# Gathers issued one by one behind pieces of work, and two gate products moved behind a layer, in a fused attention and mixture-of-experts kernel

## The chip, the cores and the metric

The kernel runs on one core of one Trainium2 chip. The metric is the time of one execution on the device in microseconds (us); of several executions the median is given. PE is the matrix engine, DVE the vector engine, ACT the scalar engine, POOL the engine that here issues the indirect transfers (gathers and scatters), SP the engine that issues the plain transfers.

## The reference, cut to what matters

A banded attention gives 3072 tokens of 512 numbers; each token then goes to one of eight experts, and its result is multiplied by a gate.

```python
x = attention(q, k, v, n_global, n_local)        # (4, 8, 768, 64) -> (3072, 512)
logits = x @ w_gate                              # (3072, 8)
expert_idx = np.argmax(logits, axis=1)
gate_w = softmax(logits)[np.arange(N), expert_idx]
for e in range(E):                               # the tokens of expert e, sorted together
    h = np.maximum(x_sorted[lo:hi] @ w1[e], 0.0) # 512 -> 1024
    y_sorted[lo:hi] = h @ w2[e]                  # 1024 -> 512
return gate_w[:, None] * y                       # y back in the tokens' order
```

Everything is in float32.

## The kernel before

`banded_attention()` computes the attention in 48 units and writes the tokens to `x_tok` in DRAM. While it ends, the tokens are counted and sorted by expert, and expert 0's work begins; then a loop goes over the eight experts (`p` from 0 to 7). The order on each engine is the order in which the code is written, since both parts stand under a manual schedule; engines wait for each other where data need it.

**Tokens of an expert** come by gathers. One gather (`gather_one`, L284) is one POOL instruction that fetches 32 tokens, as 128 rows of 128 numbers, with a list of row numbers (`rows_0`, `rows_s`). DVE then turns them (`turn_x`, L295, one transpose for a gather) into the layout that PE reads (`xe`). Expert 0 has place for 464 tokens. Its first 256 come in two halves `z` of 128 at the end of the attention; the other 208 ("the quarter", 7 gathers into `xq_0`) are worked on by the expert loop as `p = 0`. Expert 1 has place for 416 tokens, 13 gathers into `xq_s`.

**Expert 0's first 256 tokens** are a list `fill` of 16 pieces: eight of the first layer (`early_hidden`, L347, each 16 PE rows in the trace, with a relu on ACT, L349) and then eight of the second layer (`early_result`, L354, each 4 rows). `work(n)` does the next `n` pieces. The tail of `banded_attention` puts them between the steps of the sorting, so that PE has work while DVE sorts: `fetch_0(1)` makes the list of row numbers of the quarter and of expert 1 and issues the quarter's seven gathers, `order()`, `settle()`, `identify()`, `sort_acc()` and `fit()` order the other experts by their number of tokens, and `gates_of()` spreads the gates (`gslot`) to the layout of 32-token pieces (`gpc_s`, `gpc_0`): a multiplication on DVE (L276), a product on PE (L279) and a copy on DVE (L280). After the last piece of each half, `scaled()` (L335) evicts it with its gate into a tile `y`, and the scatter of that tile (L327, on POOL) is held back in the list `later`.

After the attention, `take(1)` issues expert 1's 13 gathers one after the other, and then the scatters in `later` are issued.

**The expert loop.** `ground()` (L1013 to L1019) is a check on DVE. `sort(p, part, parts)` is the transposes of an expert's gathers. `hidden(p)` is the first layer: eight products into `ph` (L1065, each 8 rows in the trace, three PSUM buffers), each with a relu on ACT (L1067). `result(p)` is the second layer; for `p = 0` it is `along_row` (four products, L1102, each evicted into `yT` by DVE, L1104, and later transposed back by PE, L1096, within `hidden(1)`); for the others L1119, with L1128 for a last rest. `fetch(p, 0)` (L256) has SP load the first weights of expert `p` as soon as `hidden(p - 2)` has ended, and `fetch(p, 1)` (L1044) the second weights after `result(p - 2)`.

From expert 2 on the gathers are not issued at once: `plan(p)` puts them in the list `pending`, and `pace(n, after)` issues the next `n` of them so that each waits for the instruction `after`, a relu or an eviction of the expert that is being worked on:

```python
def pace(n, after):
    for _ in range(min(n, len(pending))):
        behind(gather_one(*pending.pop(0)), after, "spreads the gathers over the experts' work")
```

Of the kernel before, what the change touches and what calls it, by code (L numbers as in the profile page):

```python
# [8 lines left out]
F32 = mybir.dt.float32  # L9
# [7 lines left out]
P = 128  # L17
# [6 lines left out]
NQ = 4  # L24
# [5 lines left out]
def kernel(  # L30
# [241 lines left out]

    def gates_of(pool, ps, nm, ns, gs, to):

        mg = pool.tile([P, NS, TB], F32, tag="mw", name="mg" + nm, bufs=1)[:, 0:ns, :]
        nc.vector.tensor_tensor(out=mg, in0=gs.rearrange("p (s o) -> p s o", o=1).to_broadcast([P, ns, TB]),  # L276
                                in1=grp.rearrange("p (o g) -> p o g", o=1).to_broadcast([P, ns, TB]), op=ALU.mult)
        pg = ps.tile([P, NS * TB], F32, tag="m", name="pg" + nm)[:, 0:TB * ns]
        nc.tensor.matmul(pg, lhsT=sel, rhs=mg.rearrange("p s g -> p (s g)"), start=True, stop=True)  # L279
        nc.vector.tensor_copy(out=to, in_=pg)  # L280

# [6 lines left out]
    def gather(xq, cols, n, top=N):  # L288
        for i in range(n):
            gather_one(xq, cols, i, top)  # L290
# [8 lines left out]
    def plan(p):  # L299
        if p < E:  # L300
            r = ORDER[p] - 2
            xqs[p] = xq_s[p % 2]
            cols = rows_0[1][:, 2 * TB:] if p == 1 else rows_s[:, NQ * TB * r:NQ * TB * r + NQ * TB]
            for i in range(pieces_of(CAPS[ORDER[p]])):
                pending.append((xqs[p], cols, i))

# [4 lines left out]
    def pace(n, after):  # L311

        for _ in range(min(n, len(pending))):
            behind(gather_one(*pending.pop(0)), after, "spreads the gathers over the experts' work")

    def take(p):
        plan(p)
        while pending:
            gather_one(*pending.pop(0))

# [21 lines left out]
    def hidden_0(ph, q, f0, nf):  # L342

        for f in range(nf):
            c0 = P * (f0 + f)
            for kc in range(KC):
                nc.tensor.matmul(ph[:, P * f:P * f + P], lhsT=w1_0[:, 0, kc, c0:c0 + P], rhs=xe_0[:, kc, P * q:P * q + P],  # L347
                                 start=(kc == 0), stop=(kc == KC - 1))
        nc.scalar.activation(hT_0[q][:, f0:f0 + nf, :], ph.rearrange("p (f s) -> p f s", f=nf), AF.Relu)  # L349

    def result_0(po, q, f0, nf, later=None):

        for fc in range(f0, f0 + nf):
            nc.tensor.matmul(po, lhsT=hT_0[q][:, fc, :], rhs=w2_0[:, 0, fc, :],  # L354
                             start=(fc == 0), stop=(fc == FC - 1))
        if f0 + nf == FC:
            scaled(f"y_0_{q}", P, po, gslot_0[0][:, q:q + 1], idx_0[0][:, q:q + 1], later)

    def distances(dist, kpos, loc):
# [16 lines left out]
    def banded_attention():  # L376
        with ExitStack() as actx:
# [271 lines left out]
            def fetch_0(i):  # L649

                rows_of(ps_m, f"_0{i}", LOTS[i], st.pop(("w", i)), rows_0[i])
                for h in range(2):
                    n = TB if i == 0 else pieces_of(C0) - TB * h
                    gather(xq_0[h], rows_0[i][:, TB * h:TB * h + TB], min(n, TB), N - S if i == 0 else N)

# [7 lines left out]
            def early_hidden(z, f0):  # L663
                ph = ps_s.tile([P, 2, 512], F32, tag="s", name=f"ph_0_{z}_{f0}")
                hidden_0(ph[:, 0, 0:2 * P], z, f0, 2)

            def early_result(z, f0):
                if f0 == 0:
                    st["po"] = ps_o.tile([P, DM], F32, tag="o", name=f"po_0_{z}")
                result_0(st["po"], z, f0, 2, later)  # L670

# [5 lines left out]
            def work(pieces):  # L677

                for _ in range(pieces):
                    do, z, f0 = fill.pop(0)  # L680
                    do(z, f0)

# [143 lines left out]
            sort_acc(1, gslot_s)  # L826
            work(1)
            gates_of(gp, ps_m, "_s", NR * NQ, gslot_s.rearrange("p r q -> p (r q)"), gpc_s)
            gates_of(gp, ps_m, "_1", LOTS[1], gslot_0[1], gpc_0)
            fit()  # L830
            work(2)
            turn_x(xe_0, xq_0[0], TB)
# [166 lines left out]
    with tc.manual_schedule():  # L999
        banded_attention()  # L1000

        take(1)
        while later:
            later.pop(0)()


        r2 = recips.rearrange("p a b -> p (a b)")
# [15 lines left out]
        with ExitStack() as ectx:  # L1023
# [31 lines left out]
            def hidden(p, between=None):  # L1055
# [6 lines left out]
                for fc in range(FC):  # L1062
# [5 lines left out]
                    if fc < 2 and between:  # L1068
                        between(2 * fc, 2 * fc + 2)
                    pace(1 if fc < FC - 1 else len(pending), done)  # L1070

# [14 lines left out]
            def along_row(p, C, w2t, hT):  # L1086
# [12 lines left out]
                for dc in range(KC):  # L1099
                    po = ps_o.tile([P, DM], F32, tag="po", name=f"po_{p}_{dc}")  # L1100
                    for fc in range(FC):
                        nc.tensor.matmul(po[:, 0:C], lhsT=w2t[:, 0, fc, P * dc:P * dc + P], rhs=hT[:, fc, 0:C],  # L1102
                                         start=(fc == 0), stop=(fc == FC - 1))
                    pace(2 if dc == 0 else 1, nc.vector.tensor_copy(out=yT[:, dc, :], in_=po[:, 0:C]))  # L1104
                return turn

# [25 lines left out]
            ground()  # L1132
            sort(1, 0, 1)
            hidden(0)
            fetch(2, 0)
            plan(2)
# [77 lines left out]
```

## Time and profile before

| what | value |
|---|---|
| median of 16 runs | 531.52 us (529.99 to 534.02) |
| the profiled execution's own time | 530.79 us |
| its span in the profile | 528.8 us |
| PE busy in the span | 503.4 us (95%) |
| DVE busy | 182.0 us (34%) |
| ACT busy | 127.4 us (24%) |
| POOL busy | 139.2 us (26%) |
| mean granted clock of PE | 0.988 of full speed |

The page cuts the span into 40 slices, 13.2 us each, and gives the busy share of each engine in tenths; its row PEclk is the clock granted to PE. Rows of the timeline give the start, the length, the engine, the line, the operation, its tiles and shapes, and in brackets the idle time of the engine before it with what ended it. "Remote" stands there when the profile shows no event to put the end of a wait down to. "Issue" is time in which the engine waited for nothing that the profile shows. The ends of PE's rows are modelled.

### The profile page before, as it was taken

What the parts mean: (1) busy time and instruction counts of PE and PEld (TensorE: products, weight loads), DVE (VectorE), ACT (ScalarE), POOL (GpSimd) and SP (SyncE); (2) the same over time, 40 slices, a digit from 0 to 9 for tenths busy, and PEclk for the clock granted to TensorE, in tenths of its full rate; (3) what the DMA queues carried; (4) which work ended last, traced back from release to release, by engine and by line L of the source; (5) the groups of instructions that cost most, each with busy time, mean ns of one, the idle gap of its engine ahead of it and who ended that gap; (6) DMA issues with size and microseconds to landing.
All of it is one profiled execution on the core that took longest, in us unless ns stands there. A gap on an engine that the chain in (4) does not pass through costs nothing.

```text
span 528.8 us, 7971 instructions
## 1 busy us (share of the span) xinstructions
PE 503.4 (95%) x3108; PEld 346.6 (66%) x3108; DVE 182.0 (34%) x484; ACT 127.4 (24%) x227; POOL 139.2 (26%) x161
## 2 busy tenths in 40 slices
PE   3899999999999978999999999999999999999992
PEld 2899999999988935975455446545545846545540
DVE  4787797896874423210120020030011011020010
ACT  2776656654641100101001101100100201101100
POOL 5000000000033375243344145335124525310010
PEclk9999999999999979999999999999999999999997
DMA  8989998999918911590815445173372585110000
GB/s 140 161 151 174 232 168 159 240 186 166 324 38 226 258 46 50 118 280 26 193 60 190 115 115 209 45 162 111 122 166 73 198 188 197 32 41 17 1 34 29
DMA packets 145184, 71.95 MB, mean 136 GB/s; under 512 B 126672, under 2 KB 126678, under 8 KB 145136
## 3 DMA queue, kind: packets, MB, share of 16 engines
q1 hardware_dynamic: 137344, 58.16, 48.0%
q0 software_dynamic: 5264, 12.59, 7.4%
q10 hardware_dynamic: 2528, 0.59, 0.7%
q8 instruction: 26, 0.43, 0.4%
q14 instruction: 22, 0.18, 0.1%
HBM read 59.00 MB, written 12.75 MB: 136 GB/s over the span
## 4 chain that ended last, share of the span: by engine, by line
PE 87%; another core or an unknown queue 5%; DVE 4%; DMA 1%; issue 1%; ACT 0%; SPq 0%; POOL 0%; POOLq 0%; ACTq 0%; DVEq 0%
PE ph L1065 28%; PE po L1119 26%; PE o L542 13%; PE s L507 8%; PE px L559 3%; PE ph L347 2%; PE po L1102 2%; PE pt L1128 1%; PE pq L573 1%; DMA num_w<-in_n_local_dram 1%; PE pi L632 1%; DMA vt<-in_v_dram 1%; DVE num_f L79 1%; DVE w_second L524 0%
## 5 line engine op out<-in xcount | busy, mean ns | idle before, releaser
L1067 ACT ACTIVATE hT<-ph 128x416 f32<-128x416 f32 (+4 forms) x64 | 29.5, 467 | 286.6 <-PE ph L1065 175.6
L284 POOL DMA_INDIRECT xq_s<-x_tok,rows_s x72 | 72.6, 1008 | 64.7 <-ACT hT L1067 38.3
L335 DVE TENSOR_SCALAR y<-po,gslot_s 128x512 f32<-128x512 f32 (+1 forms) x17 | 12.8, 751 | 201.1 <-PE po L1119 201.1
L1065 PE MATMUL ph<-xe,w_second 128*128 128x416 f32 (+3 forms) x256 | 79.5, 471 | 0.0
L1065 PE MATMUL ph<-xe,w_first 128*128 128x208 f32 (+3 forms) x256 | 76.7, 458 | 1.8 <-issue 1.4
L1119 PE MATMUL po<-w_second,hT 128*128 128x512 f32 (+1 forms) x176 | 76.2, 592 | 0.0
L1065 PEld LDWEIGHTS ph<-xe,w_second 128*128 128x128 f32 x256 | 48.2, 190 | 29.5 <-issue 10.4
L1065 PEld LDWEIGHTS ph<-xe,w_first 128*128 128x128 f32 x256 | 47.5, 190 | 30.1 <-issue 12.8
L1119 PE MATMUL po<-w_first,hT 128*128 128x512 f32 (+1 forms) x144 | 62.3, 592 | 0.0
L1119 PEld LDWEIGHTS po<-w_second,hT 128*128 128x128 f32 (+1 forms) x176 | 33.2, 189 | 41.3 <-issue 40.7
L284 POOL DMA_INDIRECT xq<-x_tok,rows x15 | 16.8, 1119 | 163.2 <-DVE rows L271 159.3
L542 PE MATMUL o<-vt,e 128*128 128x128 f32 x288 | 53.2, 275 | 0.0
L327 POOL DMA_INDIRECT out_dram<-y,idx_s x17 | 17.2, 1010 | 124.6 <-DVE xe L295 71.7
L1119 PEld LDWEIGHTS po<-w_first,hT 128*128 128x128 f32 (+1 forms) x144 | 27.2, 189 | 34.0 <-issue 33.5
L542 PE MATMUL o<-va,e 128*128 128x128 f32 x240 | 46.6, 276 | 0.9 <-DVE recips L546 0.9
L542 PEld LDWEIGHTS o<-vt,e 128*128 128x128 f32 x288 | 42.4, 192 | 0.1
L507 PE MATMUL s<-qT,kT 64*128 64x128 f32 x384 | 38.5, 285 | 2.3 <-ACT qT L444 2.3
L513 ACT ACTIVATE e<-s 128x1024 f32<-128x1024 f32 (+1 forms) x36 | 33.4, 948 | 27.8 <-PE s L507 27.4
L542 PEld LDWEIGHTS o<-va,e 128*128 128x128 f32 x240 | 36.4, 192 | 1.1 <-issue 1.0
L507 PE MATMUL s<-qT,kA 64*128 64x128 f32 x320 | 34.1, 291 | 2.0 <-ACT kA L428 2.0
L507 PEld LDWEIGHTS s<-qT,kT 64*128 64x128 f32 x384 | 30.1, 196 | 3.5 <-ACT qT L444 2.7
L524 DVE TENSOR_TENSOR e<-e,Wb 128x1024 f32<-128x1024 f32 x24 | 28.8, 1212 | 10.3 <-ACT e L513 10.0
(189 smaller groups left out, 507.8 us busy)
## 6 DMA issues: line engine op xcount, KB each, us to landing
w_second<-in_moe_w_dram SPq DMA_DIRECT2D x16, 512.0 KB
w_second<-in_moe_w_dram SPq DMA_DIRECT2D x4, 2048.0 KB
x_tok<-xr SPq DMA_DIRECT2D x24, 256.0 KB
w_first<-in_moe_w_dram SPq DMA_DIRECT2D x12, 512.0 KB
w_first<-in_moe_w_dram SPq DMA_DIRECT2D x3, 2048.0 KB
vt<-in_v_dram SPq DMA_DIRECT2D x31, 192.0 KB
w_second<-in_q_dram SPq DMA_DIRECT2D x60, 96.0 KB
w_second<-in_k_dram SPq DMA_DIRECT2D x60, 96.0 KB
```

Of the source, the lines that this page charges most:

```text
L284: return nc.gpsimd.indirect_dma_start(out=xq[:, i, :], out_offset=None, in_=x_tok[0:NJ * top, :], in_offset=bass.IndirectOffsetOnAxis(ap=c ...
L327: p = nc.gpsimd.indirect_dma_start(out=to[:, :], out_offset=bass.IndirectOffsetOnAxis(ap=where, axis=0), in_=y[0:rows, :], in_offset=None, ...
L335: done = nc.vector.tensor_scalar(out=y[0:rows, :], in0=po[0:rows, :], scalar1=gs[0:rows, :], scalar2=None, op0=ALU.mult)
L347: nc.tensor.matmul(ph[:, P * f:P * f + P], lhsT=w1_0[:, 0, kc, c0:c0 + P], rhs=xe_0[:, kc, P * q:P * q + P], start=(kc == 0), stop=(kc == ...
L507: nc.tensor.matmul(ps[:, h, P * m:P * m + P], lhsT=lhsT, rhs=qT[r, P * i:P * i + P], start=True, stop=True)
L513: nc.scalar.activation(e[:, :, 0:w], ps[:, :, 0:w], AF.Exp, scale=D ** -0.5)
L524: nc.vector.tensor_tensor(out=eh, in0=eh, in1=W[:, 2 * j:2 * j + 2, P:3 * P].rearrange("p h (o c) -> p h o c", o=1).to_broadcast([P, 2, 2, ...
L542: nc.tensor.matmul(po[:, t, h, :], lhsT=pt[:, h, P * m:P * m + P], rhs=(vt if own else va)[:, c0:c0 + P], start=(m == mine[0][0]), stop=(m ...
L559: nc.tensor.transpose(px[:, 2 * i + t, :], xrs[b, c][:, t, P * j:P * j + P], ident)
L1065: nc.tensor.matmul(ph[:, 0:C], lhsT=w1t[:, 0, kc, P * fc:P * fc + P], rhs=xe[:, kc, 0:C], start=(kc == 0), stop=(kc == KC - 1))
L1067: done = nc.scalar.activation(hT[:, fc, 0:C], ph[:, 0:C], AF.Relu)
L1119: nc.tensor.matmul(po[0:rows, :], lhsT=hT[:, fc, P * q:P * q + rows], rhs=w2t[:, 0, fc, :], start=(fc == 0), stop=(fc == FC - 1))
```

## The change

- `gates_of` no longer does everything at once. It multiplies on DVE into a tile of its own and returns `rest`, which does the product and the copy. It is called in the expert loop, after `ground()`; `rest` is called after `hidden(0)`.
- `fetch_0(1)` puts the quarter's seven gathers into `pending`, issues two of them at once, and plans expert 1's 13 behind them. `work()` calls `pace(1, ...)` after each piece, so each piece of PE's work lets one gather go. The rest goes behind the relus of `hidden(0)`, one behind each; the last relu no longer lets all that are pending go when `p` is 0. `take` is gone.
- `work(1)`, the two `gates_of` and `work(2)` in the tail become one `work(3)` after `fit()`.
- Expert 1's transposes, in one go ahead of `hidden(0)` before, go in two parts behind the second and the third eviction of `along_row`. The two scatters held back in `later` follow them there, one each.

```diff
-    def gates_of(pool, ps, nm, ns, gs, to):
-        mg = pool.tile([P, NS, TB], F32, tag="mw", name="mg" + nm, bufs=1)[:, 0:ns, :]
+    def gates_of(pool, nm, ns, gs, to):
+        mg = pool.tile([P, ns, TB], F32, tag="mg" + nm, name="mg" + nm, bufs=1)
         nc.vector.tensor_tensor(out=mg, ..., op=ALU.mult)
-        pg = ps.tile([P, NS * TB], F32, tag="m", name="pg" + nm)[:, 0:TB * ns]
-        nc.tensor.matmul(pg, lhsT=sel, ...)
-        nc.vector.tensor_copy(out=to, in_=pg)
+        def rest(ps):
+            pg = ps.tile([P, DM], F32, tag="pt", name="pg" + nm)[:, 0:TB * ns]
+            nc.tensor.matmul(pg, lhsT=sel, ...)
+            nc.vector.tensor_copy(out=to, in_=pg)
+        return rest
...
             def fetch_0(i):
                 for h in range(2):
                     n = TB if i == 0 else pieces_of(C0) - TB * h
-                    gather(xq_0[h], rows_0[i][:, TB * h:TB * h + TB], min(n, TB), N - S if i == 0 else N)
+                    for k in range(min(n, TB)):
+                        pending.append((xq_0[h], rows_0[i][:, TB * h:TB * h + TB], k, N - S if i == 0 else N))
+                if i == 0:
+                    while pending:
+                        gather_one(*pending.pop(0))
+                else:
+                    for _ in range(2):
+                        gather_one(*pending.pop(0))
+                    plan(1)
...
                 for _ in range(pieces):
                     do, z, f0 = fill.pop(0)
-                    do(z, f0)
+                    pace(1, do(z, f0))
...
             sort_acc(1, gslot_s)
-            work(1)
-            gates_of(gp, ps_m, "_s", NR * NQ, gslot_s.rearrange("p r q -> p (r q)"), gpc_s)
-            gates_of(gp, ps_m, "_1", LOTS[1], gslot_0[1], gpc_0)
             fit()
-            work(2)
+            work(3)
             turn_x(xe_0, xq_0[0], TB)
             turn_x(xe_0[:, :, P:2 * P], xq_0[1], pieces_of(C0) - TB)
             work(4)
...
         banded_attention()
-        take(1)
-        while later:
-            later.pop(0)()
...
-                    pace(1 if fc < FC - 1 else len(pending), done)
+                    pace(1 if fc < FC - 1 or p == 0 else len(pending), done)
...
                     pace(2 if dc == 0 else 1, nc.vector.tensor_copy(out=yT[:, dc, :], in_=po[:, 0:C]))
+                    if 0 < dc < KC - 1:
+                        sort(1, dc - 1, KC - 2)
+                        later.pop(0)()
...
             ground()
-            sort(1, 0, 1)
+            spread_gates = [gates_of(hp, "_s", NR * NQ, ..., gpc_s),
+                            gates_of(hp, "_1", LOTS[1], gslot_0[1], gpc_0)]
             hidden(0)
+            for do in spread_gates:
+                do(ps_t)
             fetch(2, 0)
             plan(2)
             turn = result(0)
```

## The prediction

> **What bounds the kernel now.** I read the page first, for the engine that is busy nearly always and the slices where it is not. Its rows over 40 slices of 13.2 us:
>
> ```profile
> PE   3899999999999978999999999999999999999992
> PEclk9999999999999979999999999999999999999997
> ```
>
> PE is the bound: outside the first slices and the last one it is below 9 only in slices 14 and 15 (185 to 211 us), and its clock dips in slice 14. So I asked for that stretch in steps of 5 us; columns are busy time of PE, PEld, DVE, ACT, POOL with counts, then granted clock, DMA share, GB/s:
>
> ```profile
> 180.00:185.00 5.00, 5.00 (x32) 3.79 (x31) 1.39 (x5) 0.77 (x2) 3.78 (x5) 1.00 0.77 273
> 185.00:190.00 5.00, 1.96 (x7) 0.74 (x5) 2.05 (x9) 0.00 (x0) 3.78 (x5) 0.87 0.11 32
> 190.00:195.00 5.00, 5.00 (x8) 2.36 (x9) 1.03 (x7) 0.00 (x0) 3.78 (x5) 0.50 0.20 52
> 195.00:200.00 5.00, 5.00 (x12) 2.12 (x11) 1.37 (x5) 0.00 (x0) 3.85 (x4) 0.95 0.18 52
> 205.00:210.00 5.00, 3.32 (x16) 2.44 (x15) 0.75 (x2) 0.53 (x3) 1.02 (x1) 1.00 0.19 66
> ```
>
> PE stands in 185:190, runs "busy" at half clock in 190:195 (8 rows in 5 us) and stands again in 205:210, while POOL issues gathers without a break (3.78 of every 5 us). The timeline of PE names the rows (start, length, line, shape, count, idle before):
>
> ```profile
> 184.34 1.91 PE L354 MATMUL po<-w_first,hT 128*128 128x512 f32 x4
> 186.95 0.46 PE L279 MATMUL pg_s<-mg_s,sel 128*128 128x96 f32 x2 [0.71 <-DVE gslot_s L722]
> 189.75 0.62 PE L279 MATMUL pg<-mg,sel 128*128 128x24 f32 x2 [2.33 <-issue]
> 190.20 13.18 PE L354 MATMUL po<-w_first,hT 128*128 128x512 f32 x24
> 203.22 3.86 PE L1065 MATMUL ph<-xe,w_first 128*128 128x208 f32 x21
> 209.86 7.30 PE L1065 MATMUL ph<-xe,w_first 128*128 128x208 f32 x40 [0.25 <-ACT hT L1067]
> ```
>
> A matmul in fp32 shows as two rows. The two gate products (L279) stand between pieces of expert 0's second layer, and PE waits for DVE around them. The timeline of all engines shows why that takes so long, and why PE stands again before 209.86:
>
> ```profile
> 189.35 0.26 DVE L280 COPY gpc_s<-pg_s 128x96 f32<-128x96 f32 x1 [2.45 <-remote]
> 209.25 0.75 DVE L335 TENSOR_SCALAR y<-po,gslot 128x512 f32<-128x512 f32 x1 [8.49 <-remote]
> 209.47 0.81 ACT L1067 ACTIVATE hT<-ph 128x208 f32<-128x208 f32 x3 [26.21 <-remote]
> ...
> 277.14 0.39 SPq L1044 DMA_DIRECT2D w_second<-in_moe_w_dram  x1
> 277.15 0.35 DVE L1083 TENSOR_SCALAR y_p<-pt,gpc 128x128 f32<-128x128 f32 x1 [3.90 <-remote]
> ```
>
> The gate product ends at 187.41 by its rows, but DVE's copy of it starts 1.9 us later. The last product of the second layer ends at 203.4, its eviction starts at 209.25, and the three relus that were ready from 204.8 on start together at 209.47. Two engines go on within 0.22 us, so it was not DVE that was held but word of PE's work that came late. The same at 277: the piece product ended at 274.35, and SP and DVE, which both wait for it, go on at 277.14 and 277.15. In all these places POOL is in a run of gathers or scatters. What holds the word back, no row shows.
>
> **The change, part by part.** All of it lies in one stretch, from the first row of the second layer (182.42) to the start of expert 0's second product, L1102, at 217.16 (the chain of waits). What PE must do there: 32 rows of L354 at 0.429 us (L1119's 48 such rows take 20.60 us in the chain) is 13.73; the row-number product (184.14 to 184.34) 0.20; 64 rows of L1065 at 0.1825 (40 in 7.30) is 11.68; the gates' two products, from the like pairs of L270 (0.20 and 0.14), 0.34. Sum 25.95 us. The stretch takes 34.74, so 8.79 us are lost, in three places. The gates: PE's piece ends at 186.06 and the next begins at 190.20, 4.14 less 0.34 of work, 3.80. The clock: 24 rows from 190.20 to 203.22 take 13.02 for 10.30, 2.72. The late relus: 24 rows from 203.22 to 209.86 take 6.64 for 4.38, 2.26.
>
> *Gates.* They leave the second layer; their DVE multiplications come after `ground()`, their products after the whole first layer of expert 0's quarter, their copies before the first `yT` copy. No PE row waits for DVE inside the layer any more: the 3.80 go, and with them the clock's 2.72, since the clock fell only after that idle time. The 0.34 of products are paid later and are in my sum. Cover: the multiplications are done by about 201 (eviction after 196.4, some 2.3 us of `ground`, 0.4 of their own), 7 us ahead of need; separate buffers let both products go back to back.
>
> The Trainium skill ("TensorE: Matmul & The Clock Gate", Part 1) has the clock halve after about 3.4 us of idle and return after about 3.4 us of work. Halving after this idle time agrees (0.50 from 189 on), but here the half clock lasts to 195.4; by the page's return the clock's term would be an estimated 1.7, and the time 1.0 us longer than I forecast.
>
> *Second half of expert 0's tokens.* Two gathers go at once, five behind pieces of PE work. PE's pieces last 1.72 us, a gather holds POOL for 1.00 plus 0.30 to the next, so POOL keeps up. The seventh goes behind the piece that ends at 187.8 (187.06 before); a gather issued at 163.49 let its transpose start at 166.05, 2.56 later, so this one lands at about 190.4, and the seven transposes (1.46) are done by 192. PE needs them at 182.42 + 13.73 + 0.20 = 196.35. Cover: 4.3 us, and beyond it each us costs one.
>
> *Expert 1's 13 gathers.* Five go behind pieces (to 196.5), eight behind the relus, one each 1.46 us. Since each is issued after a piece or relu is reported done, POOL is idle for 0.4 to 0.7 us between them and the long run is broken. Behind a waiting gather stand on POOL only more gathers and the two scatters. I take the late relus' 2.26 as gone. Bounds: nothing gone, or all; PE has three `ph` buffers, so a relu may be 2.5 us late at no cost; at 277, after a short run, the word was 2.8 late.
>
> *What is late next.* The first layer ends at 208.03, and at about 208.2 SP, whose queue order is unchanged, issues the load of expert 2's first weights (L256), which waits for just that. The thirteenth gather waits for the last relu and goes at about 208.6: 0.4 us behind the load. The trace has one such case: load at 251.90, gather at 252.69. In the DMA queues' view from 252.5 to 262 (packets, MB, share) the software queue, with a gather's 128 packets and a scatter's asked for, moves 31:
>
> ```profile
> q1 hardware_dynamic: 498, 1.85, 94.1%
> q0 software_dynamic: 31, 0.05, 2.9%
> ```
>
> So it lands when the load is through. The first load (issued 217.20) moves 0.30 MB to 220 and 1.77 MB from 220 to 229, so it takes 11.9 us; here it ends at 220.1. Its transpose (0.27) lets expert 1's first layer start at about 220.5, where PE is ready at 208.03 + 0.34 + 11.25 (L1102) + 0.12 = 219.74. I take a wait of 0.8; bounds 0 (it slips in ahead) and 3 (gathers issued at 220 to 223.5, in mid-load, show software packets mostly after 229, 14 us after the load's issue).
>
> The Trainium skill ("DMA: Bandwidth & Descriptors", Queues, rings and completion order) has each DMA engine take turns between queues packet by packet; by that the gather would land in a few us and the wait be 0. The 31 packets speak against it.
>
> *Transposes and evictions.* Expert 1's 13 transposes (2.63 at 211.64, in one go) move between the `yT` copies: 6 after the second (at about 214.2) and 7 after the third (217.1). DVE is otherwise idle there (0.38 of each 2.8 us). Behind a transposition that waits stands the fourth copy, due at 219.8; nobody needs it until PE's transposes after the first `ph`, 2.9 us on. The two scatters held back leave 205 and 210 for 214 to 218: POOL then has five gathers and two scatters, 7 × 1.3 = 9.1 us, in 11.25.
>
> *Sum.* 8.79 - 0.8 = 8.0 us off the profiled execution's own 530.79 (528.8 span and 2.0 around it), so 522.8. The runs' median, 531.52, is 0.73 above it: I predict 523.5. From 228 on PE is full to the end in the windows, so the gain is carried through.
>
> **The rivals.** *Word from PE stays late.* The gathers still run beside PE, and one run of three POOL operations at 273.5 already delays the word by 2.8. If the relus come as late as now, PE stands 2.26 again: 525.8. For: lateness without a long run. Against: it costs PE nothing at 277, with the same three buffers.
>
> *The gather slips in ahead of the load* (its descriptors are written before the load's data flows, about 1.3 us after issue): 522.7. It lies inside my forecast.
>
> *Slower: the thirteenth gather blocks DVE and PE.* Wait W is paid in full, and beyond about 3.7 us (the idle time after which the clock fell) 2.7 more for the clock. The gain is eaten when W + 2.7 = 8.8, W = 6.1: a landing at 225.6, 17 us after issue. The load would have to last 17 us instead of 11.9, and the longest in the trace is some 14. With 19 us: 533.2.
>
> *The change does not remove the idle time*, because expert 0's transposes come later than 196.35: 4.3 us of cover would have to be used up, by five gathers each late by a late word of 1 us or more. With 5 us more than the cover and the clock lost again: 531.
>
> **How the numbers follow.** Forecast with the slip 0.75, late word 0.14, idle time elsewhere 0.05, slower 0.06. The range takes the wait from 0 to 3 (522.7 to 525.7), the late word on the forecast (525.8) and with part of the wait (527), and below, 1 us for the rows' rounding and the median's own spread: 521.7 to 527. About 0.2% (1.06 us) is what a measurement of this kernel can tell from no change; faster by more 0.91, within 0.03, slower 0.06.
>
> **What would show it.** Right: clock 1.00 from 185 to 210, 24 rows of L354 in one run of 10.3 us, the first relu within 1 us of its product, L1102's successor starting near 208.4, and a wait of about 0.8 for DVE before expert 1's first `ph`. Wrong: PE idle before the first layer of the quarter (cover used up), the first relu still us behind its product (late word), or over 3 us before expert 1's `ph` (the load).

## The result, and the profile after

The changed kernel takes 520.97 us, median of 11 runs (518.75 to 522.94), against 531.61 us for the kernel before in the same series: ratio 0.9793, 95% interval 0.9776 to 0.9809. Forecast were 523.5 us, with a range from 521.7; the time lies 0.7 us below its low end. The profiled execution takes 520.62 us (span 518.8), where 522.8 was worked out.

The rows of PE and of its clock over the 40 slices, from the page of the changed kernel:

```profile
PE   3899999999999999999999999999999999999993
PEclk9899999999999999999999999999999999999998
```

Slices 14 and 15 are full, and the clock's dip is gone. The same stretch in steps of 5 us (busy time of PE, PEld, DVE, ACT, POOL with counts, then clock, DMA share, GB/s):

```profile
185.00:190.00 5.00, 5.00 (x13) 2.28 (x12) 2.11 (x11) 0.00 (x0) 2.21 (x3) 1.00 0.11 29
190.00:195.00 5.00, 5.00 (x13) 2.21 (x12) 1.20 (x7) 0.00 (x0) 3.31 (x4) 1.00 0.14 39
205.00:210.00 5.00, 5.00 (x32) 5.00 (x31) 0.35 (x2) 0.69 (x2) 2.98 (x3) 1.00 0.40 118
```

PE does 13 rows from 190 to 195 where it did 8. Its timeline:

```profile
181.78 1.88 PE L354 MATMUL po<-w_first,hT 128*128 128x512 f32 x4
183.69 12.21 PE L354 MATMUL po<-w_first,hT 128*128 128x512 f32 x28
195.74 11.42 PE L1066 MATMUL ph<-xe,w_first 128*128 128x208 f32 x64
207.36 11.50 PE L1103 MATMUL po<-hT,w_first 128*128 128x208 f32 x64
219.73 3.06 PE L1066 MATMUL ph<-xe,w_second 128*128 128x416 f32 x8 [0.76 <-issue]
```

The second layer and the first layer of the quarter are one row each, with no idle time in brackets. From the start of L354 to the start of the quarter's second product it is 25.58 us (181.78 to 207.36). By the same rows of the kernel before it was 34.58 us:

```profile
182.42 1.88 PE L354 MATMUL po<-w_first,hT 128*128 128x512 f32 x4
...
217.00 11.42 PE L1102 MATMUL po<-hT,w_first 128*128 128x208 f32 x64
```

One wait is new, 0.76 us before expert 1's first layer. The timeline of the other engines shows the eviction and the first relu on time, and where the wait comes from:

```profile
195.94 0.75 DVE L334 TENSOR_SCALAR y<-po,gslot 128x512 f32<-128x512 f32 x1 [4.74 <-PE po L354]
197.47 0.34 ACT L1068 ACTIVATE hT<-ph 128x208 f32<-128x208 f32 x1 [14.86 <-issue]
206.83 0.71 ACT L1068 ACTIVATE hT<-ph 128x208 f32<-128x208 f32 x2 [2.11 <-PE ph L1066]
207.19 1.96 SPq L256 DMA_DIRECT2D w_first<-in_moe_w_dram  x4
208.74 1.00 POOL L288 DMA_INDIRECT xq_s<-x_tok,rows  x1 [0.30 <-issue]
219.36 0.31 DVE L299 STREAM_TRANSPOSE xe<-xq_s 128x128 f32<-128x128 f32 x1 [1.73 <-DMA xq_s<-x_tok,rows]
```

The relus keep PE's step up to the seventh, which starts 1.1 us after its product's end and back to back with the eighth (206.83). The last two gathers wait for these two relus, so the thirteenth goes at 208.74, 1.55 us behind the load, and its transpose waits for it until 219.36.

What is left of the 10 us lies outside the stretch. The changed kernel is 0.65 us ahead already at 159 us, in code that is the same; and it ends faster. The last scatter of the kernel before (span 528.8 us), and then of the changed one (span 518.8 us):

```profile
520.56 0.95 POOL L327 DMA_INDIRECT out_dram<-y,idx_s  x1 [5.88 <-DVE y L335]
```
```profile
511.95 0.95 POOL L326 DMA_INDIRECT out_dram<-y,idx_s  x1 [5.89 <-DVE y L334]
```

From this row to the end of the span it is 8.2 us before and 6.9 after. The trace has POOL go from one closing instruction to the next after a gap of 1.3 us before (524.67 to 525.99) and 0.03 after, and the queue that fetches instructions has one packet more before than after:

```profile
q14 instruction: 22, 0.18, 0.1%
```
```profile
q14 instruction: 21, 0.17, 0.1%
```

### The profile page after: what moved, and what is told of

It reads as the page before. It is cut to its first block, busy times and chain, and to the rows that moved or that the text cites. A ratio compares the mean times of both kernels' runs of the same rounds, so it can differ in the third digit from the quotient of the medians.

```text
span 518.8 us, 7988 instructions
## 1 busy us (share of the span) xinstructions
PE 499.4 (96%) x3108; PEld 345.5 (67%) x3108; DVE 182.2 (35%) x484; ACT 127.0 (24%) x227; POOL 138.0 (27%) x161
## 4 chain that ended last, share of the span: by engine, by line
PE 93%; DVE 3%; DMA 2%; issue 1%; ACT 0%; POOL 0%; POOLq 0%; SPq 0%
PE ph L1066 30%; PE po L1123 26%; PE o L543 14%; PE s L508 8%; PE po L354 3%; PE px L560 3%; PE ph L346 2%; PE po L1103 2%; PE pt L1132 1%; PE pq L574 1%; DMA vt<-in_v_dram 1%; DMA num_w<-in_n_local_dram 1%; PE pi L633 1%; DVE num_f L79 1%; DVE w_second L525 0%
## 5 line engine op out<-in xcount | busy, mean ns | idle before, releaser
L1066 PE MATMUL ph<-xe,w_second 128*128 128x416 f32 (+3 forms) x256 | 79.6, 471 | 0.8 <-issue 0.8
L1066 PE MATMUL ph<-xe,w_first 128*128 128x208 f32 (+3 forms) x256 | 75.8, 457 | 0.1
L1066 PEld LDWEIGHTS ph<-xe,w_second 128*128 128x128 f32 x256 | 48.2, 190 | 30.4 <-issue 11.3
L1066 PEld LDWEIGHTS ph<-xe,w_first 128*128 128x128 f32 x256 | 47.5, 190 | 27.6 <-issue 10.7
```

The lines of the kernel that those rows point to most:

```text
L1066: nc.tensor.matmul(ph[:, 0:C], lhsT=w1t[:, 0, kc, P * fc:P * fc + P], rhs=xe[:, kc, 0:C], start=(kc == 0), stop=(kc == KC - 1))
```

## The experiments

Theory A: a run of gathers that follow each other without room on POOL holds PE's word of finished work; all three losses of the stretch (round the gates, the half clock, the late relus) are that, and pacing the gathers removes them. Theory B, the prediction's own sum: the gates' idle time with the half clock, and the late relus, are separate terms.

The runs were made in five further series, each on one chip. In the first two the kernel before takes 531.9 and 532.7 us, as on record; in the last three 521.9, 521.6 and 521.6. That is a finding of its own (below); each ratio is to the kernel before in its own series. A trace can be up to 1.4 us ahead of another or behind it before the stretch begins (L559 at 153.28 in pad8_before, at 154.45 in the kernel before, at 155.84 in changed_third), so the stretch is counted from its own first row where that matters.

| run | kernel before | this | ratio (95%) |
|---|---|---|---|
| gates_only | 531.88 | 534.28 | 1.0049 (1.0032 to 1.0065) |
| gathers_only | 531.88 | 521.35 | 0.9814 (0.9795 to 0.9833) |
| four_ahead | 531.88 | 519.92 | 0.9784 (0.9765 to 0.9803) |
| pad8_before | 531.88 | 529.63 | 0.9964 (0.9949 to 0.9979) |
| spaced | 532.65 | 520.97 | 0.9794 (0.9762 to 0.9826) |
| run_of_8 | 532.65 | 519.87 | 0.9764 (0.9737 to 0.9792) |
| attn_gathers | 532.65 | 540.19 | 1.0151 (1.0118 to 1.0183) |
| attn_memsets | 532.65 | 520.36 | 0.9781 (0.9751 to 0.9811) |
| spaced_gates | 521.85 | 519.78 | 0.9960 (0.9944 to 0.9976) |
| spaced_short | 521.85 | 520.35 | 0.9971 (0.9959 to 0.9983) |
| run_of_8_again | 521.85 | 519.25 | 0.9951 (0.9934 to 0.9967) |
| changed_again | 521.85 | 519.58 | 0.9961 (0.9948 to 0.9973) |
| before_again | 521.59 | 521.77 | one run |
| spaced_short_again | 521.59 | 520.51 | 0.9981 (0.9966 to 0.9996) |
| changed_third | 521.59 | 519.41 | 0.9962 (0.9943 to 0.9980) |
| run_of_8_third | 521.59 | 519.07 | 0.9953 (0.9937 to 0.9970) |
| spaced_short_third | 521.62 | 520.90 | 0.9978 (0.9962 to 0.9994) |
| gates_only_again | 521.62 | 520.67 | 0.9978 (0.9960 to 0.9996) |

### The gates alone, the gathers alone

```diff
# gates_only, against the kernel before; gates_of as in the change
...
-            work(1)
-            gates_of(gp, ps_m, "_s", ...)
-            gates_of(gp, ps_m, "_1", ...)
             fit()
-            work(2)
+            work(3)
...
             ground()
+            spread_gates = [gates_of(hp, "_s", ...), gates_of(hp, "_1", ...)]
             sort(1, 0, 1)
             hidden(0)
+            for do in spread_gates:
+                do(ps_t)
```

> The kernel before with the gates' part of the change alone: their multiplications after ground(), their products and copies after hidden(0), the pieces in one work(3); the 20 gathers stay in one run without a pause, and expert 1's transposes and the two held-back scatters stay where they were. Theory A (word of PE's work comes only when POOL's run of gathers ends, whatever PE does): the second layer's 32 rows run in one piece to about 196.4, PE fills its three ph buffers by about 200.6 and then stands until the relus' word comes at 207 to 209, as before; expert 0's second product still starts at 215 to 217, and the kernel gains 0 to 2 us (529.5 to 531.6), although the gates' idle time and the half clock behind them are gone or have moved. Theory B (the three losses are separate terms, as the prediction's sum has them): 3.80 and 2.72 go, the relus' 2.26 stays: about 525.1, ratio 0.988.

Measured: slower by half a per cent, 534.28 us. The timeline of PE in gates_only, and then that of the other engines:

```profile
184.93 12.21 PE L359 MATMUL po<-w_first,hT 128*128 128x512 f32 x28
196.97 4.38 PE L1067 MATMUL ph<-xe,w_first 128*128 128x208 f32 x24
211.63 9.15 PE L1067 MATMUL ph<-xe,w_first 128*128 128x208 f32 x40 [10.28 <-ACT hT L1069]
```
```profile
205.85 1.02 POOL L332 DMA_INDIRECT out_dram<-y,idx  x1 [0.30 <-issue]
206.79 0.75 DVE L340 TENSOR_SCALAR y<-po,gslot 128x512 f32<-128x512 f32 x1 [12.71 <-remote]
...
207.82 1.16 POOL L332 DMA_INDIRECT out_dram<-y,idx  x1 [0.95 <-DVE y L340]
...
211.24 0.81 ACT L1069 ACTIVATE hT<-ph 128x208 f32<-128x208 f32 x3 [27.46 <-remote]
```

The second layer runs in one piece, as theory B has it, and nothing is won by it. Its last product ends at 197.1, and DVE evicts it only at 206.79, as POOL's run ends (206.87). PE fills its three `ph` buffers and stands 10.28 us; the relus come at 211.24, behind one more scatter. Against before the second product starts 3.98 us later, which is 1.77 (relus at 211.24 instead of 209.47), 1.85 (40 rows in 9.15 instead of 7.30, since after such idle time the clock is 0.50) and 0.36 for the gates' products. Of the 1.77, 0.59 is that the layer itself begins later in this trace (183.01 for 182.42); counted from there the stretch is 3.39 us longer (37.97). The gain of removing the gates' idle time was paid back at the next wait, which lasts to the run's end. The word is not held for the whole run, though: the first half is evicted at 191.95, in its middle. Theory A forecast that the gain would be gone, though not that it would turn into a loss.

Half clock costs 2.1 us on these 40 rows (7.04 at the 0.176 of the row after). By the granted clock in steps of 1 us (0.79 in 215:216, and 0.74 in 195:196 before) it lasted 3.8 us from PE's restart here, and 5.3 us in the kernel before. The Trainium skill ("TensorE: Matmul & The Clock Gate", Part 1) has the clock return after about 3.4 us of sustained work; both are longer here.

gathers_only is the reverse: the changed kernel with the gates back in `work(1)`, gates, `fit()`, `work(2)`.

```diff
# gathers_only, against the changed kernel; gates_of as before, spread_gates gone
...
+            work(1)
+            gates_of(gp, ps_m, "_s", ...)
+            gates_of(gp, ps_m, "_1", ...)
             fit()
-            work(3)
+            work(2)
```

> The changed kernel with the gates' multiplications, products and copies back between the pieces of expert 0's second layer, in work(1), gates, work(2); the gathers one by one behind pieces and relus, transposes and scatters as in the changed kernel. Theory A (the idle time round the gates was mostly late word of PE's work too): the copy of the first gate product starts within 1 us of its end instead of 1.9, PE's idle time between the pieces falls from 3.80 to 2 or less, the clock stays at 1.00, and the relus are on time: 523 to 525. Theory B (the idle time round the gates is the chain over DVE, whatever POOL does): idle 3.8 and half clock 2.7 stay, only the relus' 2.26 goes, less the 0.8 for the thirteenth gather: about 530.

Measured 0.9814, theory A. PE's timeline in gathers_only:

```profile
185.47 0.46 PE L279 MATMUL pg_s<-mg_s,sel 128*128 128x96 f32 x2
186.37 0.40 PE L279 MATMUL pg<-mg,sel 128*128 128x24 f32 x2 [0.44 <-DVE mg L276]
186.61 10.55 PE L350 MATMUL po<-w_first,hT 128*128 128x512 f32 x24
197.00 11.42 PE L1065 MATMUL ph<-xe,w_first 128*128 128x208 f32 x64
208.25 11.42 PE L1102 MATMUL po<-hT,w_first 128*128 128x208 f32 x64
```

The gates stand where they stood, and PE is idle round them for about half a us (0.11 and 0.44) instead of 3.80; no half clock follows. The stretch takes 26.71 us (181.54 to 208.25): 7.87 of the 9.00 us come from the gathers, with the transposes and scatters that move along with them, and 1.13 from the gates.

### Is it the run, and of what?

```diff
# spaced, against the kernel before: the seven gathers of fetch_0(1) likewise
     def take(p):
         plan(p)
         while pending:
             gather_one(*pending.pop(0))
+            nc.gpsimd.memset(pad, 0.0)          # 256 columns
```

> The kernel before with a memset of 256 columns (some 0.3 us) on POOL behind each of the 20 gathers of the quarter and of expert 1; nothing waits for PE. POOL stays busy without a pause, but a gather starts only every 1.6 us instead of 1.3, and the run ends some 6 us later. Theory A (as long as gathers follow each other with no wait for PE in between, PE's word comes only behind the run): the first relu comes 6 us later than before, PE stands longer, and the kernel is 4 to 7 us slower (ratio 1.008 to 1.013). Theory B (gathers that follow each other at POOL's highest rate hold the word; a little room lets it through): relus on time, gain of 2 to 8 us (0.985 to 0.996).

Measured 0.9794: 20 memsets on the busy engine, with nothing else changed, bring what the whole change brings. (In both, about 1.3 us of that are the end of the kernel, below. The stretch takes 26.78 us in spaced, 181.80 to 208.58, as in gathers_only.) The timelines of POOL and ACT in spaced:

```profile
196.55 1.01 POOL L284 DMA_INDIRECT xq_s<-x_tok,rows  x1 [0.17 <-issue]
197.56 0.33 POOL L321 MEMSET pad<- 128x256 f32 x1
198.05 1.00 POOL L284 DMA_INDIRECT xq_s<-x_tok,rows  x1 [0.17 <-issue]
...
199.06 0.34 ACT L1072 ACTIVATE hT<-ph 128x208 f32<-128x208 f32 x1 [16.68 <-PE ph L1070]
200.34 0.34 ACT L1072 ACTIVATE hT<-ph 128x208 f32<-128x208 f32 x1 [0.94 <-PE ph L1070]
```

A gather starts every 1.49 us instead of 1.30, POOL never pauses, nothing waits for PE, and the relus come in PE's step, beside the run. So it is not the wait for PE that helps, nor POOL's leisure. Whether the 0.19 us or the other instruction does it was to be told by a memset of one column, with a gather still every 1.30 us:

> The kernel before with a memset of one column on POOL behind each of the 20 gathers, in place of 256 columns, so that a gather starts about every 1.3 to 1.4 us. Theory A (the word needs room in time between the gathers; 0.19 us more from one to the next was enough in the run spaced): with little room the word is late again, at least in part: 0.985 to 1.003. Theory B (another instruction between two gathers is what lets it through): 0.978 to 0.981.

> The kernel before with a memset of one column on POOL behind each of the 20 gathers; a gather still starts every 1.30 us. Where the kernel before takes about 531.5 us: theory A (the word needs room in time): late as in the kernel before, ratio 0.995 to 1.003; theory B (another instruction between two gathers lets it through): 0.978 to 0.981. Where the kernel before takes about 522 us it tells nothing, ratio 0.997.

> The kernel before with a memset of one column behind each of the 20 gathers, a gather still every 1.30 us. Where the kernel before takes about 531.5 us: theory A (the word needs room in time): 0.995 to 1.003; theory B (another instruction between two gathers lets it through): 0.978 to 0.981. Where it takes about 521.7 us: 0.997 to 0.998 again, nothing told.

All three fell into series in which the word is not late in the kernel before either; they tell nothing, and this stays open. What they gain, 0.7 to 1.5 us, is about the gap at the end, which none of them has.

The same run elsewhere, and its control, both in the changed kernel (20 unused gathers, or 18 memsets, behind an exponential of the attention at about 105 us):

```diff
+                if n0 == 30:
+                    for i in range(20):
+                        one = nc.gpsimd.indirect_dma_start(out=xq_s[i // 13][:, i % 13, :], in_=<128 rows of moe_w2>, ...)
...
+                    for i in range(18):
+                        one = nc.gpsimd.memset(xq_s[i // 9], 0.0)
```

> The changed kernel with 20 gathers added that nobody uses (128 rows of 128 numbers of the second weights, into the tiles that experts 1 and 2 are gathered into later), in one run on POOL from about 105 us, in the attention, where PE, ACT and DVE wait for each other every few us and POOL has nothing to do. Theory A (a run of gathers holds PE's word, wherever it is): PE's word comes late there too, and since a unit of the attention needs it every 3 us, the kernel is 5 to 20 us slower (ratio 0.989 to 1.018). Theory B (the word is held by something of the stretch around 200 us, not by the run): within 1 us of the changed kernel (0.978 to 0.981).

> The control for the gathers in the attention: the changed kernel with 18 memsets of 1.49 us added on POOL at the same place, 27 us in one run without a DMA. Theory A1 (gathers hold PE's word, POOL's work as such does not): within 1 us of the changed kernel (0.978 to 0.981). Theory A2 (any run of POOL's does, or it takes DVE's access to memory): several us slower, as with the gathers.

The changed kernel has 0.9793. With the memsets it is 0.9781, no difference; with the gathers 1.0151, 19.8 us more than with the memsets on the same chip. Windows of attn_gathers, then of attn_memsets:

```profile
115.00:120.00 5.00, 4.18 (x45) 3.47 (x43) 2.74 (x3) 1.14 (x2) 3.78 (x5) 1.00 1.07 203
120.00:125.00 5.00, 3.12 (x11) 2.33 (x12) 0.00 (x0) 0.00 (x0) 3.78 (x5) 0.65 1.30 205
```
```profile
120.00:125.00 5.00, 5.00 (x58) 4.76 (x57) 3.25 (x6) 2.60 (x4) 4.83 (x5) 1.00 1.04 189
```

From 120 to 125 DVE and ACT do nothing at all while POOL gathers, and PE does 11 rows for 58. POOL's memsets, as long and as dense (4.83 of 5 us), disturb nobody. That it is word of PE here too, and not the loads of the attention, shows in ACT's timeline of attn_gathers: the scores that this exponential reads come from PE alone, their last row ended at 116.45, and ACT takes them up 9.6 us later, after standing idle for 7.51.

```profile
126.04 1.02 ACT L516 ACTIVATE w_second<-s 128x1024 f32<-128x1024 f32 x1 [7.51 <-remote]
```

PE itself is held as well: from 119.6 on its rows start singly, some 0.7 us apart (119.60, 120.32, 121.03), with idle time that the profile puts down to issue. In the kernel before three rows of the first layer start like that too (207.77, 208.47, 209.17).

So it is the gathers, not POOL's being busy, and not something of the place around 200 us. Whether it is their issuing on POOL or what they move, these runs do not separate.

### How long a run is harmless, and the thirteenth gather

```diff
# run_of_8, against the changed kernel
-                    pace(1, do(z, f0))
+                    pace(1 if fill else len(pending), do(z, f0))
# four_ahead, against the changed kernel
-                    for _ in range(2):
+                    for _ in range(4):
                         gather_one(*pending.pop(0))
```

> The changed kernel, but the last piece of expert 0's second layer lets all eight remaining gathers go at once, instead of one behind each relu of the first layer. Theory A (the relus were on time after the change only because each gather waits for a relu): the run of eight, from about 196 to 206.6, holds PE's word of the first products; the first relus come at 207 to 209, PE stands from about 200, ratio 0.990 to 0.996. Theory B (it takes the longer run of before, more than ten gathers, to hold the word): relus within 2.5 us of their products, PE does not stand, and since the thirteenth gather is now ahead of the load, 0.978.

> The changed kernel with four instead of two gathers of the quarter issued without a wait, so that expert 1's thirteenth gather goes behind the sixth relu and not behind the last, ahead of the load of expert 2's first weights. Theory A (the 0.76 us that PE stands before expert 1's first layer is this gather queued behind the load): all 20 gathers are issued by about 206, ahead of the load, the wait is gone, ratio 0.978 to the kernel before (520.2) where the changed kernel has 0.9793. Theory B (a gather is late through POOL's run, or the longer run at the start makes word of PE's work late): same time as the changed kernel or up to 1 us longer (0.979 to 0.981).

run_of_8: 0.9764. ACT's timeline:

```profile
200.66 0.34 ACT L1068 ACTIVATE hT<-ph 128x208 f32<-128x208 f32 x1 [1.06 <-issue]
202.38 0.34 ACT L1068 ACTIVATE hT<-ph 128x208 f32<-128x208 f32 x1 [1.37 <-PE ph L1066]
205.21 0.34 ACT L1068 ACTIVATE hT<-ph 128x208 f32<-128x208 f32 x1 [2.49 <-PE ph L1066]
208.08 0.34 ACT L1068 ACTIVATE hT<-ph 128x208 f32<-128x208 f32 x1 [2.52 <-PE pg L281]
```

The relus now come 1.4 us apart and then 2.8, so the run of eight does hold the word in its second half; but PE's 64 rows take 11.42 us without idle time, since three buffers cover it. Theory A was right that the word is held, though not from the first relu on, and wrong on the price, theory B the other way round. The thirteenth gather goes ahead of the load in both kernels (207.11 for 209.64, and 205.91 for 207.52 in four_ahead), and PE's wait before expert 1 is gone in both traces. four_ahead's ratio is 0.0009 below the changed kernel's, half a us, where 0.76 was expected; the intervals do not separate that from zero.

> The same kernel as in the run run_of_8 (0.9764, interval 0.9737 to 0.9792 from four executions), beside the changed kernel on the same chip. Theory A (it is faster than the changed kernel by the 0.76 us that PE stands behind the thirteenth gather, and late word inside three buffers costs nothing): 0.7 to 0.8 us less than the changed kernel, ratio 0.0014 lower. Theory B (chance): same as the changed kernel within 0.3 us.

> The changed kernel with the last eight gathers let go at once by the last piece of the second layer. Where the kernel before takes about 531.5 us: 0.7 to 0.8 us less than the changed kernel, from the wait that goes; where it takes about 522 us: the same within 0.3 us.

Beside the changed kernel, where the word is not late, run_of_8 is 0.33 and 0.34 us faster (519.25 to 519.58, 519.07 to 519.41), each time less than the intervals can tell. With 0.9764 to the 0.9793 on record it has the lowest median wherever it ran, by little and nowhere clear of the noise.

### Where the instructions lie

```diff
# pad8_before, against the kernel before, at the start of the attention
+        for _ in range(8):
+            nc.gpsimd.memset(pad, 0.0)          # one column
```

> The kernel before with eight memsets of one column added on POOL early in the attention, where POOL is idle; nothing else changes. The trace of before shows 1.3 us between the end of POOL's INC_SWDGE_SEM (524.67) and its last long DRAIN (525.99), with one more fetch of instructions (22 against 21) than after the change, where the gap is 0.03. Theory A (the gap is a fetch of POOL's instructions, and where it falls depends on how many instructions lie ahead): the gap goes or moves, and the time falls by 0 to 1.3 us (ratio 0.9975 to 1.000). Theory B (the gap belongs to the end of the kernel before, or is chance): gap and time stay (ratio 1.000), or the gap is there in some executions only. The 0.65 us that the changed kernel is ahead already at 159 us, in code that is the same, is looked at as well: if it is a matter of the run, it comes and goes in the traces of these four kernels.

Measured 0.9964, 2.2 us by the medians. The gap at the end is gone (0.04 us), with 21 packets of instructions for 22. The 22 packets recur in all four traces of the kernel before and of gates_only, with a gap of 1.2 to 1.3 us, and in none of the other 16 traces. So about 1.3 us of the change's gain come from where POOL's instructions lie, and not from what they do. That the gap goes with the packets is shown; that it is the fetch itself is argued from the one packet. PE's timeline of pad8_before also shows the run's end at work again:

```profile
180.16 1.88 PE L354 MATMUL po<-w_first,hT 128*128 128x512 f32 x4
...
185.23 10.55 PE L354 MATMUL po<-w_first,hT 128*128 128x512 f32 x24
...
207.34 9.35 PE L1068 MATMUL ph<-xe,w_first 128*128 128x208 f32 x40 [4.34 <-ACT hT L1070]
```

Here the word of the gates' products happened to come early: the idle time round them is 0.44 us and the clock stays full, and by the start of the next row of L354 PE is 5.0 us ahead of before (185.23 for 190.20). Of these 2.3 were there when the layer began (180.16 for 182.42), and 2.7 are won at the gates. All but 0.5 us is lost again: the second half, whose last row ended at 195.8, is evicted at 206.73, the first relus come at 206.95, 2.9 us after the run's end (204.05; 3.2 us before), and the second product starts at 216.53 (217.00 before). Counted from its first row the stretch is 1.8 us longer than before (36.37).

### Where the word is not late

> The kernel before, unchanged. Theory A (late word of PE's work shows on some chips only): where the runs of before take about 531.5 us, the trace has the idle time at 185 to 190 and 205 to 210, half the clock in between, and the first relus 3 to 6 us behind their products; where they take about 522 us, the same gathers run at the same 1.30 us, and the relus follow their products within 0.1 us. Theory B (the kernel before was faster there for another cause, such as the start, the loads or the end): the lateness is there in either case.

> The changed kernel itself, beside the others on the same chip: 0.979 again. Its trace shows whether the lead of 0.65 us at 159 us, in unchanged code, and the missing gap at the end come again. Theory A (the gap goes with where the instructions lie): no gap in this trace either. Theory B (chance): gap and lead may be there or not.

> The changed kernel, beside the others on the same chip: 0.979 where the kernel before takes about 531.5 us, 0.996 where it takes about 522 us. In the first case PE stands 0.76 us before expert 1's first layer, in the second not, since with timely relus the thirteenth gather goes ahead of the load.

> The gates' part of the change alone, as in the run gates_only, with the memset of 256 columns behind each of the 20 gathers. Theory A (the gates' idle time was late word too, and what is left of it once the gathers are spaced is about 0.6 us): 0.978 to 0.979, half a us less than with spacing alone (0.9794), although the same move made the kernel slower (1.0049) while the gathers ran without room. Theory B (moving the gates costs something by itself, as gates_only showed): 0.981 to 0.985.

> The kernel of the run gates_only again. Where the kernel before takes about 531.5 us: 1.005 again. Where it takes about 521.7 us: PE's idle time round the gates is 0.5 us there (185.30 to 185.41 and 185.87 to 186.31 in the trace of before_again), and that is the gain, 0.9985 to 0.9995, with the gap at the end still there.

The kernel before, unchanged, takes 521.6 to 521.9 us in these series. From its page, then the timeline of POOL and ACT, then that of PE:

```profile
PE   3999999999999999999999999999999999999992
PEclk9999999999999999999999999999999999999997
```
```profile
196.56 1.00 POOL L284 DMA_INDIRECT xq_s<-x_tok,rows  x1 [0.30 <-DMA xq_s<-x_tok,rows]
...
198.67 0.34 ACT L1067 ACTIVATE hT<-ph 128x208 f32<-128x208 f32 x1 [16.61 <-PE ph L1065]
199.95 0.34 ACT L1067 ACTIVATE hT<-ph 128x208 f32<-128x208 f32 x1 [0.94 <-PE ph L1065]
```
```profile
186.31 0.40 PE L279 MATMUL pg<-mg,sel 128*128 128x24 f32 x2 [0.44 <-DVE mg L276]
196.93 11.42 PE L1065 MATMUL ph<-xe,w_first 128*128 128x208 f32 x64
```

The same 20 gathers run at the same 1.30 us, and no relu is late. By the times of PE's semaphore updates in the ten traces of these three series, one word of PE's comes more than 0.3 us after its product (0.9 us, in spaced_short); in the kernel before on record 22 do, in the changed kernel 18. The stretch takes 26.71 us (181.48 to 208.19), to the hundredth what gathers_only reaches where the word is late. So pacing does all that a chip without this lateness would do, and no more.

What is left there is 0.9961 and 0.9962, 2.2 us: 1.13 of the stretch, which is the gates (26.71 to 25.58 in gates_only_again, 0.9978, 0.95 us by the medians, twice what was expected from the idle time alone), and the gap at the end, 1.2 to 1.3. spaced_gates and the changed kernel are equal there (519.78, 519.58); its stretch takes 25.57 us without idle time, but what it gains over a late kernel before, its question, was not to be had. PE's wait before expert 1 is 0.17 us in changed_third and none in changed_again, but not because the thirteenth gather goes ahead of the load, as was expected: it goes 0.62 us behind it in both (208.74 for 208.12, 207.34 for 206.72).

Whether the chip decides, or the time at which it was used, the runs do not tell: each of the five series was on a chip of its own.

## Why the prediction was right and wrong

**The stretch.** Forecast was 8.79 us, measured 9.00; 64 rows of L1066 take 11.25 instead of 11.68, and the two gate products 0.37 instead of 0.34. Clock, one run of rows, first relu 0.3 us behind its product: the signs named came, with the second product starting 1.0 us ahead of the time named (207.36 for 208.4).

**Why it goes.** Here the working was wrong in a way that the sum did not show. "No PE row waits for DVE inside the layer any more: the 3.80 go, and with them the clock's 2.72" put 6.52 us down to moving the gates. Alone that brings a loss of 2.4 us where the word is late, and a gain of 1.1 in the stretch (0.95 by the medians) where it is not. The idle time round the gates was itself late word, and three waits with one cause were added like three causes. They cannot be taken away one by one: as long as the run stands, the next wait reaches its end. Only because the change breaks the run too did the sum come out; that its parts add up to the right stretch is luck to that extent.

**Late relus taken as gone** was right, for the reason given: the run is broken. The rival that the word stays late from short runs was half true: in the changed kernel the seventh relu is 1.1 us late, and at 268 the word is 2.8 late as before; the buffers cover it.

**The wait behind the load**: 0.8 forecast, 0.76 measured, and four_ahead and run_of_8, where the gather goes ahead of the load, have none. In gathers_only, 0.62 us behind the load (209.06 for 208.44), the transpose waits as well, to 219.30, but PE, ready only then, does not. One reading of the prediction is wrong: a gather is not 128 packets here but 32 (the software queue moves 32 in each of 240:241, 243:244, 246:248 and 248:250 in the trace of before), so the 31 packets would nearly be one gather. That it is kept waiting is right all the same: from 253 to 258 that queue moves none, nor from 209 to 212 in the changed kernel. The gather needed 10.6 us from its issue to its transpose. By the rule of the Trainium skill ("DMA: Bandwidth & Descriptors", Queues, rings and completion order) that queues take turns packet by packet it would have landed in a few us, by an estimate; the measurement decides. The rivals with a longer wait, or with the idle time unchanged, did not come. (The 533.2 for 19 us comes out at 533.5 by its own terms; nothing hangs on it.)

**The cover of 4.3 us** for the quarter's tokens held: the seventh gather goes at 187.59 (187.8 forecast) and PE does not wait before 195.74.

**The step that failed** is the sentence that all of the change lies in one stretch, with the carry-over "From 228 on PE is full to the end in the windows, so the gain is carried through" and a low end of the range of 1 us "for the rows' rounding and the median's own spread". 2.0 us of the profiled execution's gain lie outside. About 1.4 of them are the end of the kernel, put at nothing in the sum: 1.3 is the gap on POOL, which pad8_before shows to be a matter of where POOL's instructions lie. The other 0.65 are there at 159 us. Beside the first eight gathers, ACT takes up at 156.12 scores whose last row ended at 154.5, in the changed kernel 0.64 us earlier (155.48). Between the same two transposes of PE (L559, 154.45 to 160.96) the execution of before on record takes 6.51 us and the changed kernel 5.81; gates_only, gathers_only, four_ahead, before_again, changed_again and changed_third, with the same code up to that point, take 5.40 to 5.78, the kernel before itself among them (5.40). So it was most likely a late word of the execution that was profiled, which the change does not touch. The last 0.4 of the miss is that the changed kernel's median lies only 0.35 us above its profiled execution, where 0.73 was carried over from before; no trace shows where the other executions of the kernel before spend their time, so that stays open. What a change of instructions does at the kernel's end was priced at nothing because no row of PE shows it.

## What to carry to other kernels

When several engines wait on one engine while another runs a dense series of indirect DMAs, look at when its word arrives, not at each wait: waits with a common end are one term, and removing one of them only lengthens the next. Break the series, by waits or even by a memset of 0.33 us between its instructions, and measure on more than one chip, since the lateness may not be there on the next. Leave a us or so in the range for the end of the kernel when the number of POOL's instructions changes.

## What the runs showed of the hardware that was not expected

- A run of gathers on POOL, one every 1.30 us, kept word of finished PE work back by up to 10.9 us (ended 195.8, taken up at 206.73 in pad8_before; 9.7 in gates_only); with one every 1.49 us and a memset in between the relus beside the run came at once (199.06, 200.34 in spaced). What holds it, no trace shows.
- The same kernel shows this in some series and not at all in others: 531.5 to 532.7 us and 521.6 to 521.9 us, with the same gathers at the same pace.
- 18 memsets of 1.49 us on POOL beside the attention cost nothing; 20 gathers cost 20 us.
- Eight unrelated memsets on POOL, some 500 us ahead, take 1.3 us off the end of the kernel (pad8_before: a gap of 0.04 us for 1.3, 21 packets of instructions for 22).
